# First MLP's output forms built from words held in SBUF, with own buffers for combining sums and an order planned with 315 GB/s of DMA

## The chip, the cores and the metric

The kernel runs on one core of a Trainium2 chip. Its metric is the device time of one execution in microseconds. The kernel before took 1105.91 us, the median of three runs (1105.8 to 1106.16).

## What is computed

Chunked attention (32 queries see 8 memory slots and a window of 56 keys and values) over 4 x 768 tokens and 8 heads is followed by two MLPs, 512 to 2048 to 512 wide, on all 3072 tokens. The inputs are float32; the kernel takes the weights of both MLPs as 64-bit words.

```python
for c in range(nc):
    scores = scale * np.matmul(q_c, k_full.transpose(0, 1, 3, 2))
    a = np.exp(scores - np.max(scores, axis=-1, keepdims=True))
    a = a / (np.sum(a, axis=-1, keepdims=True) + 1e-09)
    out[:, :, c_start:c_end] = np.matmul(a, v_full)
x = out.transpose(0, 2, 1, 3).reshape(B * S, H * D)
h = x @ w_in;  x = (h * (1.0 / (1.0 + np.exp(-h)))) @ w_out
h = x @ w2_in; r = np.maximum(h, 0.0); y = (r * r) @ w2_out
```

## The kernel before

**Numbers.** Every float32 operand of a matmul is kept as a high and a low part, and a product is three matmuls (low by high, high by low, high by high). A weight arrives as 64-bit words in a tile `wraw`; `words` makes a float32 tile `wu` of it with two passes on ScalarE (L621, L626, the second into a tile `wr`) and two on VectorE (L630, L636). `high` and `low` then split `wu` into the two parts.

**Stages.** The 3072 tokens are six blocks of 512. In the first two blocks the first MLP runs plainly (`mlp`: `hidden` L947 to L949, `back` L992 to L994); meanwhile its weights are converted (`convert`, block 0) and stay in SBUF: `w_in` in `i0` to `i15`, `w_out` as high and low parts in `o0` to `o9`, `u0` to `u2`. In the other four blocks (`first`, `front1`) the product with `w_out` is a block scheme with seven products for eight, per pair of 128-wide slices of the hidden layer: the sums of the left side are made per pair (`sums`, `split`), and the right side ("forms") is prepared once. The second MLP (`second`, `front`, `visit`) uses such a scheme for both of its products; its forms are prepared while the first MLP runs.

**The first MLP's output forms.** In `convert`, `keep_words` (L723) stores the `wu` tile of every `w_out` slice to the DRAM tensor `w1s` in two halves. In block 1, `convert_out(0, k)`, for each of the eight pairs k, loads the words of its two slices back into `wu` tiles (L759, four loads a pair), makes four differences (`diff`, L777), and stores the results to `w1s` (L824). `load_pair` (L1431) later loads a pair's six forms for each of the four blocks; the seventh form of all pairs is fetched by `hold_fourth` (L1403), split once into `o3` to `o6`, and the parts are stored to `w1h` (L1413), from where the last of the four blocks is served.

**The second MLP's weights.** Sixteen jobs, eight `stage_forms` and eight `convert_second` in turn, each load two `wraw` tiles, make words and differences, and store forms (`w2i` L891, `w2s` L811; seven stores of 256 KB in a `convert_second`). Which pair's step starts a job stands in `WORK0` for block 1 and in `WORK` for the blocks after it; in a block of `first` a job is due `LATER` = 20 us behind the step's time.

**Combining.** After a block of the seven-product scheme `combine` adds the products up from PSUM: a copy on ScalarE (L1484), then additions on VectorE (L1489), into four tiles of the pool `wr`, which `words`, the differences and the evictions of the first two blocks use too.

**What sets the order.** Nothing is issued when it is written: every step is a `Piece` with costs per engine, a due time, what it follows, the buffers it makes and uses, and `Graph.order` plans all of them with a list scheduler and emits them in the planned order, which fixes the order of every engine's queue. An engine runs its queue strictly in order, so an instruction that waits holds up all behind it. SyncE ("SP") issues all transfers. In the planner a transfer takes its bytes at `PIPE` MB/us on one pipe and lands `LANDING` us later; a step with two engines allowed goes to the cheaper one that is free.

```python
PIPE, LANDING, SPARE, DENSE, QUEUE = 0.34, 1.9, 3.0, 40.0, 1.5
...
pipe = max(pipe, p.end) + p.size / self.PIPE / 1e6
p.end = pipe + self.LANDING
```

Of the kernel before, what the change touches and what calls it, by code (L numbers as in the profile page):

```python
# [13 lines left out]
F32 = mybir.dt.float32  # L14
# [6 lines left out]
ALU = mybir.AluOpType  # L21
# [12 lines left out]
DM = H * D  # L34
DFF = 2048
P = 128
# [3 lines left out]
ON_PE = 2  # L40
AHEAD, SOON, SLOP = 15.0, 12.0, 2.0
FORMS1, FORMS2, LATER = (1, 2, 4, 5, 7), (0, 2, 4), 20
WORK0, WORK = (2, 4, 6), ((0, 1, 3, 4, 5), (2, 3, 4, 5), (2, 3, 4, 5))
UC = UG * GC // 2
QW, KW, VW = UC * CHUNK, UC * KC, UC * (D + 1)
UW = QW + KW + VW
# [10 lines left out]
HALF2 = T2 // 2  # L57
PAIRS = FT // 2
# [41 lines left out]
class Graph:  # L100
    HOP, DRAIN = 0.15, 0.2
    TABLE = 1.3
    PIPE, LANDING, SPARE, DENSE, QUEUE = 0.34, 1.9, 3.0, 40.0, 1.5

    def __init__(self):
        self.pieces, self.tags = [], {}
# [126 lines left out]
def chunk_attention_two_mlps(ctx, tc, units, weights, out):  # L233
# [17 lines left out]
        pool(tag)  # L251
    for tag, n in (
        ("rq", 1), ("rv", 2), ("pr", 1), ("pts", 1), ("xq", 3), ("x0", 1), ("x1", 1), ("g", 3), ("wraw", 2),
        ("wu", 4), ("wr", 4), ("nm", 3), ("sm", 4),
    ):
        pool(tag, n)
    for tag, n in (("acc", 4), ("ph", 2), ("sc", 2)):
# [2 lines left out]
    y1 = dram.tile([KT, P, NT], F32, name="y1")  # L260
    bounce = dram.tile([(NB - ON_PE) * HP * 2, P, GC, UG * CHUNK], F32, name="bounce")
    turns = iter(range((NB - ON_PE) * HP * 2))
    w1s = dram.tile([PAIRS, P, NF + 1, HALF2], F32, name="w1s")
    w1h = dram.tile([PAIRS, P, 2, HALF2], F32, name="w1h")
    w2i = dram.tile([PAIRS, P, NF, HALF2], F32, name="w2i")
    w2s = dram.tile([PAIRS, NF, P, 2, HALF2], F32, name="w2s")
# [1 line left out]
    def f(ap):  # L268
        return ap.bitcast(F32)

    def take(b, shape, dtype, name=None):
        b.tile = pools[b.tag].tile(shape, dtype, tag=b.tag, name=name or b.tag)
        return b.tile
# [379 lines left out]
    def convert(i, c):  # L653
# [64 lines left out]
        if c:  # L718
            w_kept[i] = []
            for half, part in enumerate(PLACES[i % 2]):  # L720
                def keep_words(e, half=half, part=part):
                    hs = slice(half * HALF2, (half + 1) * HALF2)
                    nc.sync.dma_start(out=w1s[i // 2, :, part], in_=wu.tile[:, hs])  # L723

                w_kept[i].append(G.add({"SP": 0.45}, due + 4, keep_words, [d], uses=[wu],
                                       size=P * HALF2 * 4))
# [17 lines left out]
    def convert_out(l, k, due):  # L744

        got, stored = {}, []
        for n in range(2):
            if l:
                wraw, at = load_words(k + n * PAIRS, 1, due)
                at.release = due - 25  # L750
                wu, at = words(1, k + n * PAIRS, 1, due, wraw, 0, at)
                got[n] = wu, [at]
            else:
                wu, i, at = G.buf("wu"), 2 * k + n, []
                for half, place in enumerate(PLACES[n]):
                    def load(e, wu=wu, half=half, place=place):
                        t = wu.tile if half else take(wu, [P, DM], F32)
                        hs = slice(half * HALF2, (half + 1) * HALF2)
                        nc.sync.dma_start(out=t[:, hs], in_=w1s[k, :, place])  # L759

                    at.append(G.add({"SP": 0.45}, due - 6, load, [*w_kept[i], *at[:half]],
                                    new=[wu] * (1 - half), uses=[wu] * half, size=P * HALF2 * 4))
                    at[-1].release = due - 12
                    stored.append(w_kept[i][half])
                got[n] = wu, at
        (ua, da), (ub, db) = got[0], got[1]
        z = [G.buf("wr"), G.buf("wr")]
# [4 lines left out]
        def diff(to, left, right, after, new):  # L772

            def emit(e):
                if new:
# [3 lines left out]
                )  # L779

            return G.add({"DVE": 0.42, "POOL": 0.75}, due + 1, emit, after, port=True,
                         new=[z[to[0]]] * new, uses=[ua, ub] + [z[to[0]]] * (not new))

        def b(src, half):
            return lambda: halves(src.tile)[:, half]
# [610 lines left out]
    def hold_fourth(due):  # L1396
        for k in range(0, PAIRS, 2):
# [14 lines left out]
            def store(e, k=k, w=w):  # L1412
# [3 lines left out]

            w_half[k] = [G.add({"SP": 0.45}, due + 40 + k, store, [d], uses=[w],
                                   size=4 * P * HALF2 * 4)]
            for i in range(2):
                held_fourth[k + i] = (w, i, d)  # L1420

# [52 lines left out]

    def combine(b, due):

        y = [G.buf("wr") for _ in range(4)]
        t1, u2, u3, y22 = y

        def done(n):  # L1480
# [288 lines left out]
```

## Time and profile before

| | us |
|---|---|
| median of 3 runs (1105.8 to 1106.16) | 1105.91 |
| the profiled execution's own time | 1104.76 |
| its span, first to last instruction | 1102.7 |
| TensorE (PE) busy | 1071.5 (97% of the span) |
| VectorE (DVE) busy | 823.5 (75%) |
| ScalarE (ACT) busy | 598.2 (54%) |
| GpSimd (POOL) busy | 230.6 (21%) |
| bytes moved, mean rate | 262.96 MB, 238 GB/s |

Busy time is the union of an engine's instructions. The matmuls are pipelined, so two neighbours overlap in the records: 12 matmuls of 512 columns take 2.8 us at the full clock (one starts 0.23 us after the other) and 5.1 us at half of it (0.43 us). The granted clock is shown as a share of 2.4 GHz; 0.50 is 1.2 GHz. The program's stages by time: start, to 34 us; blocks 0 and 1 of the first MLP, to about 231 us; its four other blocks, to about 607 us; the second MLP, to the end.

### The profile page before, as it was taken

Reading aid. Unit: us, or ns where it says so; the run is one execution under the profiler, and the core shown is the slowest. Engines: PE = TensorE matmul, PEld = TensorE weight load, DVE = VectorE, ACT = ScalarE, POOL = GpSimd, SP = SyncE. Lnnn points to the kernel's source line nnn. Section 1 sums busy time; section 2 is a strip of 40 time slices with the busy share of each in tenths; the row PEclk is TensorE's granted clock in tenths of the full one; section 3 lists DMA queues with packets and bytes.
Section 4 is the critical chain, followed back from the end, with each engine's and each line's share of the span. In section 5 each row is a group of like instructions: output and inputs, shape, how many; then the busy total and the mean of one; then the engine's idle time right before and its main releaser. Section 6 shows DMA issues by size and latency. Waiting matters only on the chain.

```text
span 1102.7 us, 25401 instructions
## 1 busy us (share of the span) xinstructions
PE 1071.5 (97%) x10060; PEld 980.5 (89%) x10060; DVE 823.5 (75%) x1621; ACT 598.2 (54%) x1102; POOL 230.6 (21%) x216
## 2 busy tenths in 40 slices
PE   6899999989998999999999999999999999999998
PEld 4677777768887888888889999999999999999998
DVE  4787755548789888887987887777777777777766
ACT  2788844437866758576676444334335335334333
POOL 0111102203334223411200321311221221211200
PEclk8799999998999999999999999999999999999999
DMA  7875898998888978866854585765765765766675
GB/s 270 298 258 193 259 290 287 312 311 273 284 279 276 311 250 272 276 223 213 271 201 157 196 262 172 244 211 165 262 202 183 242 210 180 226 208 215 203 222 173
DMA packets 145814, 262.96 MB, mean 238 GB/s; under 512 B 12704, under 2 KB 57888, under 8 KB 145696
## 3 DMA queue, kind: packets, MB, share of 16 engines
q1 hardware_dynamic: 145696, 261.34, 72.5%
q8 instruction: 79, 1.29, 0.5%
q14 instruction: 39, 0.32, 0.1%
HBM read 207.81 MB, written 53.48 MB: 237 GB/s over the span
## 4 chain that ended last, share of the span: by engine, by line
PE 79%; DMA 10%; DVE 5%; issue 2%; ACT 2%; SPq 1%; POOL 0%; ACTq 0%; DVEq 0%
PE out L1325 33%; PE pp L1145 21%; PE ph L947 6%; PE ph L948 6%; PE ph L949 6%; DMA turned<-bounce 2%; DMA w1s<-t 2%; DMA w<-w1s 2%; DMA raw<-units 2%; PE po L548 1%; PE acc L992 1%; PE acc L994 1%; PE acc L993 1%; PE sc L414 1%; DMA w2i<-wr 1%
## 5 line engine op out<-in xcount | busy, mean ns | idle before, releaser
L1145 PE MATMUL pp<-xs,forms 128*128 128x256 f32 x2016 | 274.2, 282 | 0.2 <-DVE kept L1171 0.2
L1325 PE MATMUL out<-w,g 128*128 128x256 f32 x2016 | 272.9, 283 | 1.3 <-DMA w<-w2s 0.6
L1325 PEld LDWEIGHTS out<-w,g 128*128 128x128 f32 x2016 | 255.7, 191 | 1.9 <-DVE y L1489 1.1
L1145 PEld LDWEIGHTS pp<-xs,forms 128*128 128x128 f32 x2016 | 253.8, 189 | 0.4 <-DVE kept L1171 0.4
L1203 ACT CAST g<-sums 128x512 fp32r<-128x512 f32 x240 | 148.2, 618 | 125.1 <-PE out L1325 109.1
L1207 DVE TENSOR_TENSOR g<-sums,g 128x512 fp32r<-128x512 f32 x202 | 156.0, 775 | 50.6 <-ACT g L1203 49.9
L1325 PE MATMUL out<-g,w 128*128 128x256 f32 x1344 | 175.3, 286 | 5.4 <-ACT y L1484 3.1
L1325 PEld LDWEIGHTS out<-g,w 128*128 128x128 f32 x1344 | 168.7, 191 | 10.9 <-ACT y L1484 3.5
L947 PE MATMUL ph<-x,i 128*128 128x512 f32 x384 | 155.6, 405 | 5.0 <-DVE pr L498 5.0
L1162 ACT ACTIVATE sums<-pp 128x256 f32<-128x256 f32 x192 | 73.7, 384 | 159.9 <-PE pp L1145 139.8
L948 PE MATMUL ph<-x,i 128*128 128x512 f32 x384 | 153.4, 399 | 0.0
L949 PE MATMUL ph<-x,i 128*128 128x512 f32 x384 | 153.2, 399 | 0.0
L1188 POOL TENSOR_TENSOR sums<-sums 128x256 f32<-128x256 f32 x55 | 46.6, 852 | 277.8 <-DVE sums L1188 236.5
L947 PEld LDWEIGHTS ph<-x,i 128*128 128x128 f32 x384 | 73.4, 191 | 22.1 <-issue 5.4
L1181 DVE SCALAR_TENSOR_TENSOR sums<-sums 128x256 f32<-128x256 f32 x144 | 67.2, 474 | 31.6 <-ACT sums L1162 29.6
L949 PEld LDWEIGHTS ph<-x,i 128*128 128x128 f32 x384 | 73.4, 191 | 17.6
L948 PEld LDWEIGHTS ph<-x,i 128*128 128x128 f32 x384 | 73.6, 192 | 15.5
L1207 POOL TENSOR_TENSOR g<-sums,g 128x512 fp32r<-128x512 f32 x38 | 49.9, 1315 | 170.8 <-ACT g L1203 163.5
L1188 DVE TENSOR_TENSOR sums<-sums 128x256 f32<-128x256 f32 x185 | 77.5, 437 | 7.2 <-ACT sums L1285 3.7
L1382 ACT CAST w<-w 128x512 fp32r<-128x512 f32 x100 | 60.6, 617 | 39.1 <-DMA w<-w1s 26.2
L1388 DVE TENSOR_TENSOR w<-w,w 128x512 fp32r<-128x512 f32 x76 | 58.5, 780 | 24.1 <-ACT w L1382 23.6
L630 DVE SCALAR_TENSOR_TENSOR wr<-wu,wr 128x512 int32<-128x512 int32 x64 | 46.2, 732 | 19.8 <-ACT wr L626 18.0
(109 smaller groups left out, 1312.6 us busy)
## 6 DMA issues: line engine op xcount, KB each, us to landing
w<-w2s SPq DMA_DIRECT2D x120, 512.0 KB, 4.0
w<-w1s SPq DMA_DIRECT2D x32, 768.0 KB, 5.4
w<-w2s SPq DMA_DIRECT2D x96, 256.0 KB, 3.1
wraw<-weights SPq DMA_DIRECT2D x44, 512.0 KB, 5.6
raw<-units SPq DMA_DIRECT2D x20, 768.0 KB, 6.3
w2s<-ws SPq DMA_DIRECT2D x56, 256.0 KB, 3.7
raw<-units SPq DMA_DIRECT2D x20, 520.0 KB, 5.9
bounce<-squares SPq DMA_DIRECT2D x32, 256.0 KB, 4.5
```

The costliest lines, as they stand in the source:

```text
L947: nc.tensor.matmul(o, w[:, 1, ws], x[:, 0, kt], start=(kt == 0), stop=False)
L948: nc.tensor.matmul(o, w[:, 0, ws], x[:, 1, kt], start=False, stop=False)
L949: nc.tensor.matmul(o, w[:, 0, ws], x[:, 0, kt], start=False, stop=(kt == KT - 1))
L1145: nc.tensor.matmul(o[:, at], w[:, a, ws], t[:, c, kt], start=first and kt == 0 and r == 0, stop=kt == 1 and r == 2, skip_group_check=True,)
L1162: nc.scalar.activation(t[:, to], q.bank[bank].tile[:, h], func)
L1181: nc.vector.scalar_tensor_tensor(t, t, 0.0, t, op0=ALU.max, op1=ALU.mult)
L1188: engine[e].tensor_tensor(q.t.tile[:, to], a[0].tile[:, a[1]], b[0].tile[:, b[1]], op=op)
L1203: nc.scalar.copy(take(g, [P, 2, 2, HALF2], F32R, "g2")[:, :, 0], read())
L1207: engine[e].tensor_tensor(t[:, :, 1], read(), f(t[:, :, 0]), op=ALU.subtract)
L1325: nc.tensor.matmul(out_, held[:, ms], moving, start=first and r == 0 and (m == 0 or alone is not None), stop=last and r == 2, skip_group_c ...
L1382: nc.scalar.copy(take(w, [P, m, 2, HALF2], F32R, "w2")[:, :, 0], raw.tile[:, at:at + m])
L1388: engine[e].tensor_tensor(t[:, :, 1], raw.tile[:, at:at + m], f(t[:, :, 0]), op=ALU.subtract)
```

## The change

`convert_out(0, k)` no longer loads the words: `whole` adds the high and low part of `w_out`, which are in SBUF, into a `wu` tile, one instruction per slice, on VectorE or GpSimd (16 in all). The half of a slice that only this load needed is no longer stored, and `w1s` is smaller by it. `combine` takes two of its four tiles from a new pool `y` with two buffers, and `wr` goes from four to three. The stores of `w1h` may be planned 250 us behind their due time at the earliest. `PIPE` and `LANDING` become 0.315 and 2.2. Each block has four jobs for the second MLP (block 1 had three, the block after it five). The fourth difference is also marked as a user of both of its inputs' tiles.

```diff
-WORK0, WORK = (2, 4, 6), ((0, 1, 3, 4, 5), (2, 3, 4, 5), (2, 3, 4, 5))
+WORK0, WORK = (1, 3, 5, 6), ((2, 3, 4, 5), (2, 3, 4, 5), (2, 3, 4, 5))
...
-    PIPE, LANDING, SPARE, DENSE, QUEUE = 0.34, 1.9, 3.0, 40.0, 1.5
+    PIPE, LANDING, SPARE, DENSE, QUEUE = 0.315, 2.2, 3.0, 40.0, 1.5
...
-        ("wu", 4), ("wr", 4), ("nm", 3), ("sm", 4),
+        ("wu", 4), ("wr", 3), ("y", 2), ("nm", 3), ("sm", 4),
...
-    w1s = dram.tile([PAIRS, P, NF + 1, HALF2], F32, name="w1s")
+    w1s = dram.tile([PAIRS, P, NF, HALF2], F32, name="w1s")
...
             for half, part in enumerate(PLACES[i % 2]):
+                if part == NF:
+                    continue
+
                 def keep_words(e, half=half, part=part):
...
-                wu, i, at = G.buf("wu"), 2 * k + n, []
-                for half, place in enumerate(PLACES[n]):
-                    def load(e, wu=wu, half=half, place=place):
-                        t = wu.tile if half else take(wu, [P, DM], F32)
-                        hs = slice(half * HALF2, (half + 1) * HALF2)
-                        nc.sync.dma_start(out=t[:, hs], in_=w1s[k, :, place])
-
-                    at.append(G.add({"SP": 0.45}, due - 6, load, [*w_kept[i], *at[:half]],
-                                    new=[wu] * (1 - half), uses=[wu] * half, size=P * HALF2 * 4))
-                    at[-1].release = due - 12
-                    stored.append(w_kept[i][half])
+                wu, i = G.buf("wu"), 2 * k + n
+
+                def whole(e, wu=wu, i=i):
+                    w = f(out_words(i))
+                    engine[e].tensor_tensor(
+                        take(wu, [P, DM], F32), w[:, 0], w[:, 1], op=ALU.add
+                    )
+
+                at = [G.add({"DVE": 0.70, "POOL": 1.30}, due - 1, whole, [w_done[i, 1]],
+                            new=[wu], uses=[w_out[i]], port=True)]
+                at[0].release = due - 12
+                stored += w_kept[i]
...
-                         new=[z[to[0]]] * new, uses=[ua, ub] + [z[to[0]]] * (not new))
+                         new=[z[to[0]]] * new, uses=[ua, ub] + (z if to == (1, 1) else [z[to[0]]] * (not new)))
...
+            w_half[k][0].release = due + 250
...
-        y = [G.buf("wr") for _ in range(4)]
+        y = [G.buf("y"), G.buf("y"), G.buf("wr"), G.buf("wr")]
```

Since the planner lays out everything anew, instructions move on every engine. Three places follow, where TensorE waits in the profile of before. Lines of the changed kernel are numbered 3 to 5 higher.

The first is VectorE about 20 us into the first block of the seven-product scheme. `nm` and `pr` are the maxima and the scores of an attention unit, which free the two PSUM banks `sc`; `wu` and `wr` belong to a conversion for the second MLP. Before:

```order
L630 SCALAR_TENSOR_TENSOR wr_3252<-wu_3215,wr_3252 128x512
L438 TENSOR_REDUCE nm_3268<-sc_3218 128x4
L636 SCALAR_TENSOR_TENSOR wu_3215<-wu_3215,wr_3252 128x512
L630 SCALAR_TENSOR_TENSOR wr_3263<-wu_3255,wr_3263 128x512
L498 TENSOR_TENSOR pr_3284<-sc_3218,nm_3268 128x4x64
L438 TENSOR_REDUCE nm_3268<-sc_3219 128x4
L498 TENSOR_TENSOR pr_3284<-sc_3219,nm_3268 128x4x64
L636 SCALAR_TENSOR_TENSOR wu_3255<-wu_3255,wr_3263 128x512
```

The same unit in the changed kernel:

```order
L1211 TENSOR_TENSOR g2_3210<-sums_3188,g2_3210 128x2x256
L438 TENSOR_REDUCE nm_3259<-sc_3213 128x4
L498 TENSOR_TENSOR pr_3267<-sc_3213,nm_3259 128x4x64
L438 TENSOR_REDUCE nm_3259<-sc_3214 128x4
L498 TENSOR_TENSOR pr_3267<-sc_3214,nm_3259 128x4x64
L1036 COPY y_3288<-acc_2149 128x512
L604 TENSOR_TENSOR x1_3269<-turned_3191,x1_3269 128x512
```

The conversion's four instructions no longer stand among those that free the banks; that conversion is now the fourth job of block 1, and stands earlier.

The second is ScalarE at the start of the next block, where `combine` copies the first product out of PSUM (L1484, then L1489). Before:

```order
L621 ACTIVATE wu_4608<-wraw_4471 128x512
L626 ACTIVATE wr_4624<-wraw_4471 128x512
L800 CAST ws_4629<-wu_4553 128x256
L1285 ACTIVATE sums_4631<-ph_4580 128x2x256
L505 ACT_TABLE_LOAD
L505 ACTIVATE pr_4567<-pr_4567 128x512
L800 CAST ws_4639<-wu_4608 128x2x256
L1484 COPY y_4643<-out_3358 128x512
```

Changed:

```order
L621 ACTIVATE wu_4467<-wraw_4388 128x512
L1207 CAST g2_4507<-kept_3200 128x2x256
L626 ACTIVATE wr_4511<-wraw_4388 128x512
L1489 COPY y_4526<-out_3346 128x512
L1386 CAST w2_4537<-w2_4443 128x2x256
L1207 CAST g2_4547<-kept_3200 128x2x256
L1386 CAST w2_4557<-w2_4443 128x2x256
```

The copy moved from behind the second `wraw` tile of a conversion, a table load and the exponential to a place ahead of them, two `hidden` products earlier on TensorE.

The third is GpSimd at the start of the block after that: `g2` are low parts of the left side, `w2` those of the forms. Before:

```order
L1207 TENSOR_TENSOR g2_6099<-sums_5833,g2_6099 128x2x256
L1388 TENSOR_TENSOR w2_6084<-w2_5870,w2_6084 128x2x256
L1388 TENSOR_TENSOR w2_6088<-w2_5870,w2_6088 128x2x256
L1207 TENSOR_TENSOR g2_6127<-sums_5833,g2_6127 128x2x256
L1207 TENSOR_TENSOR g2_6230<-sums_5994,g2_6230 128x2x256
```

Changed:

```order
L781 TENSOR_TENSOR t_6001<-wu_5951,t_6001 128x256
L781 TENSOR_TENSOR t_6095<-wu_5951,wu_5895 128x256
L1211 TENSOR_TENSOR g2_6066<-sums_5801,g2_6066 128x2x256
L1211 TENSOR_TENSOR g2_6111<-sums_5801,g2_6111 128x2x256
L1192 TENSOR_TENSOR sums_5973<-sums_5973 128x256
L808 TENSOR_TENSOR ws_6080<-wu_5951,ws_6080 128x2x256
```

The two subtractions for the forms (now `w2_5943`, `w2_5947`) have moved to VectorE, earlier in the program, and nothing stands between the two `g2` of the block's first pair.

## Rows read from the trace of the kernel before

**Rows 1.** The page's part 1: busy us, share of the span, instructions of each engine.

```profile
PE 1071.5 (97%) x10060; PEld 980.5 (89%) x10060; DVE 823.5 (75%) x1621; ACT 598.2 (54%) x1102; POOL 230.6 (21%) x216
```

**Rows 2.** Stretches of 50 us: busy us (instructions) by engine, PE clock, DMA share, GB/s.

```profile
200.00:250.00 50.00, 45.19 (x433) 35.62 (x432) 24.20 (x53) 21.68 (x37) 6.95 (x9) 0.98 0.97 310
300.00:350.00 50.00, 46.90 (x512) 41.11 (x511) 44.57 (x85) 35.84 (x63) 16.40 (x14) 0.97 0.82 276
450.00:500.00 50.00, 46.90 (x455) 41.52 (x454) 40.27 (x85) 31.43 (x57) 11.35 (x12) 0.97 0.68 233
700.00:750.00 50.00, 50.00 (x421) 50.00 (x421) 37.17 (x72) 17.98 (x37) 10.10 (x9) 1.00 0.65 202
```

**Rows 3.** Waits of PE: line, waited for: us in total, times, longest.

```profile
PE ph L947 <- DVE pr L498: 5.0, 2, 4.8
PE sc L414 <- DVE wr L630: 3.6, 1, 3.6
PE out L1325 <- ACT y L1484: 3.1, 1, 3.1
PE out L1325 <- POOL g L1207: 2.2, 1, 2.2
```

**Rows 4.** The three short stretches at half clock behind waits, columns as in rows 2.

```profile
248.50:255.20 6.70, 5.84 (x14) 4.63 (x15) 6.03 (x11) 6.30 (x12) 3.79 (x3) 0.50 0.32 123
347.50:350.80 3.30, 3.00 (x25) 2.78 (x33) 2.62 (x5) 2.22 (x5) 0.00 (x0) 0.50 0.71 207
453.30:456.60 3.30, 3.30 (x18) 3.30 (x17) 2.35 (x6) 1.04 (x2) 0.00 (x0) 0.50 1.08 341
```

**Rows 5.** Timeline of ACT and DVE, 243 to 249 us: start, us, instruction [idle before <-releaser].

```profile
243.99 0.66 ACT L621 ACTIVATE wu<-wraw 128x512 f32<-128x512 f32 x1 [5.33 <-DMA wraw<-weights]
...
245.23 0.69 DVE L630 SCALAR_TENSOR_TENSOR wr<-wu,wr 128x512 int32<-128x512 int32 x1 [5.41 <-ACT wr L626]
...
248.19 0.69 DVE L630 SCALAR_TENSOR_TENSOR wr<-wu,wr 128x512 int32<-128x512 int32 x1 [1.33 <-issue]
```

**Rows 6.** DMA issues, whole run: out<-in, times, size, median us to landing.

```profile
w1s<-wu SPq DMA_DIRECT2D x32, 128.0 KB, 4.1
wu<-w1s SPq DMA_DIRECT2D x32, 128.0 KB, 3.9
...
w2i<-wr SPq DMA_DIRECT2D x16, 256.0 KB, 4.5
...
w1h<-w SPq DMA_DIRECT2D x4, 512.0 KB, 5.4
```

**Rows 7.** Timeline of ACT, 342 to 348 us.

```profile
342.79 0.67 ACT L621 ACTIVATE wu<-wraw 128x512 f32<-128x512 f32 x1 [1.03 <-DMA wraw<-weights]
...
347.17 0.58 ACT L1484 COPY y<-out 128x512 f32<-128x512 f32 x1
```

**Rows 8.** Timeline of POOL, 447 to 453 us.

```profile
448.77 2.53 POOL L1388 TENSOR_TENSOR w<-w,w 128x512 fp32r<-128x512 f32 x2
451.26 1.46 POOL L1207 TENSOR_TENSOR g<-sums,g 128x512 fp32r<-128x512 f32 x1
```

**Rows 9.** The start, 28 to 35 us: SP, DVE, PE timelines, then landing times of L383's loads.

```profile
28.09 0.38 SPq L383 DMA_DIRECT2D raw<-units  x1
...
31.89 0.68 DVE L604 TENSOR_TENSOR x<-turned,x 128x512 fp32r<-128x512 f32 x1
...
33.09 0.69 DVE L712 TENSOR_TENSOR i<-wu,i 128x512 fp32r<-128x512 f32 x1
...
34.45 1.17 PE L414 MATMUL sc<-raw 64*32 64x64 f32 x64 [3.65 <-DVE wr L630]
...
DMA to landing us min/median/max: 6.2/7.1/8.0
```

**Rows 10.** Groups by line: shapes, count | busy us, mean ns | idle before.

```profile
L712 POOL TENSOR_TENSOR u<-wu,u 128x512 fp32r<-128x512 f32 x4 | 5.2, 1292 | 21.7 <-ACT u L708 21.7
...
L712 DVE TENSOR_TENSOR o<-wu,o 128x512 fp32r<-128x512 f32 x3 | 2.1, 690 | 1.9 <-ACT o L708 1.9
```

**Rows 11.** Waits of ACT's word instructions: us in total, times, longest.

```profile
ACT wr L626 <- DMA w1s<-t: 3.5, 3, 2.5
```

## The prediction

> **What bounds the kernel now.** I read the shares of the engines first, then the table by stages, then PE's own waits, and last the timelines around each wait. PE is busy for 97% of the span [rows 1], and from about 610 us to the end it is busy without a break: a stretch there shows 50.00 of 50 us at the full clock [rows 2]. Nothing that this change touches can shorten that part, since the matmuls stay the same. What can be won lies where PE is not at its peak: in the start, and in the first MLP, where a few stretches are short of 50 us and of the full clock [rows 2]. The list of PE's waits names four places [rows 3], and behind three of them the clock falls from 2.4 to 1.2 GHz after PE had idled, for the time that the stretches in [rows 4] show. So a wait costs its idle time and half of the busy time at half clock.
>
> The first is the wait of a `hidden` product at 244 us for the scores of an attention unit (4.8 us, [rows 3]). The reader should see in [rows 5] why DVE was late: it was idle for 5.41 us in front of an L630, which waited for ACT, which had waited 5.33 us for a `wraw` load. The reductions that free the bank stood behind that L630 in DVE's queue. A load was late because the 16 DMA engines were busy: 0.97 of the stretch, at 310 GB/s [rows 2]. The second, at 344 us, is `combine`'s copy, which began at 347.17 us, behind the words of a `wraw` tile for which ACT had waited until 342.79 us [rows 7]. The third, at 450 us, is a `g` that GpSimd could begin only at 451.26 us, after two L1388 of 2.53 us together [rows 8]. The fourth is the start: at 34.45 us a score for block 1 went ahead of the first `hidden` product [rows 9].
>
> **The change part by part.** *Start.* The wait at 34.45 us is put down to DVE's L630, but the score reads only a load; that load was issued at 28.09 us and took at least 6.2 us to land [rows 9], so it was the load that came last. In the changed order the score stands behind the first twelve matmuls of `hidden`, and the load is issued one place earlier. `hidden` then needs the last `x` part, which ended at 31.89 + 0.68 = 32.57 us, and the low part of `w_in`, which ended at 33.09 + 0.69 = 33.78 us [rows 9]; the changed order puts the latter ahead of the former. So PE starts between 32.6 and 33.8 us in place of 34.45: 0.7 to 1.9 us, and I take 1.7, since with that swap the last `x` ends the wait.
>
> *Words kept in SBUF.* 32 loads and 8 of 32 stores of 128 KB go [rows 6]: 4.2 + 1.0 MB, that is 13.5 and 3.4 us of the DMA engines at 310 GB/s [rows 2], and 40 issues of SP's queue. Added are 16 additions of 128x512; the order has 8 on GpSimd and 8 on DVE. The nearest rows are the subtractions of the same size: 1.29 us on GpSimd, 0.69 us on DVE [rows 10]. They lie between about 135 and 230 us, where DVE works half of the time (24.20 of 50 us, [rows 2]), and are hidden; without that cover they would cost at most 8 x 0.69 = 5.5 us on DVE.
>
> *Stores of `w1h` and jobs.* The four stores of 512 KB [rows 6] leave the stretch before 250 us, 2.1 MB or 6.8 us at 310 GB/s, and go to about 465 us, where the engines are busy 0.68 of the time [rows 2]. One conversion moves from the block after 230 us to the one before it: by its shapes two loads of 512 KB and seven stores of 256 KB, 2.9 MB. Block 1 thus loses 5.2 - 2.9 = 2.3 MB (the eight dropped stores lie just before it), and the stretch from 230 us loses 2.1 + 2.9 = 5.0 MB. Together with the changed order on DVE, where no instruction that hangs on a load stands between the score and its reductions, the wait at 244 us goes: 4.8 us, and of 5.84 us at half clock [rows 4] 2.9 us: 7.7 us. Its lower bound is nothing (DVE's queue has other conversions ahead, which now belong to block 1).
>
> *Combining.* The copy takes a tile of its own pool and stands ahead of the table load and of the second tile's words. 3.1 us go [rows 3], and half of 3.00 us [rows 4]: 4.6 us. Late next would be the sums that need `wr` tiles, of which there are three now; the order has them where they were. *GpSimd at 450 us.* The two L1388 are now on DVE and earlier: 2.2 us [rows 3] and half of 3.30 us [rows 4], 3.9 us. DVE has no great reserve there (40.27 of 50 us, [rows 2]), which is why I do not count on more.
>
> *Planner's numbers.* 0.315 in place of 0.34 lies near the 310 GB/s of the full stretch [rows 2]; the planner no longer sets work that hangs on loads where they cannot have landed. No time of its own.
>
> *What comes new.* All queues are laid out anew, and between 230 and 500 us DVE is still busy for 44.57 and 40.27 of 50 us [rows 2], with conversions in ACT's and DVE's queues ahead of work that PE needs. Bounds: none, or a wait like the largest, 7.7 us, and more than once. I take one of the smallest of the three, 3.9 us.
>
> **Sum**, against the profiled execution's own 1104.76 us: 1.7 + 7.7 + 4.6 + 3.9 = 17.9 us go, 3.9 us come: 1104.76 - 17.9 + 3.9 = 1090.8 us. The median of the runs is 1.15 us above that execution, so 1091.9 us.
>
> **A rule against it.** The stretch from 200 to 250 us shows 0.97 of the engines' time at 310 GB/s [rows 2]. The Trainium skill, "DMA: Bandwidth & Descriptors", section "Bandwidth", gives 425 GB/s for one core alone with large transfers and a ceiling of 435 by its ports; by it the engines would have about a quarter to spare at 310 (an estimate from that page). The row differs: busy to 0.97; whether the transfers' size explains it no run here shows. The rule is behind the third rival below.
>
> **Rivals.** *All clean*: no new wait; 1105.91 - 17.9 = 1088.0 us. For it: block 1 and the stretch from 230 us lose 2.3 and 5.0 MB. Against it: the small waits of before came from the same queues.
>
> *The block starts stay*: the waits at 344 and 450 us have the same kind of cause, a conversion's work in front of what frees a bank, and a new order may put another one there. Only the start and 244 us are won: 1105.91 - 1.7 - 7.7 = 1096.5 us. For it: DVE's 44.57 of 50 us; against it: the order at both places.
>
> *The loads are not late for want of DMA time*: they land as late as before, with fewer bytes in flight too, and the wait at 244 us turns up behind the conversion's new place; the others go: 1105.91 - 1.7 - 4.6 - 3.9 = 1095.7 us. Against it stands the 0.97. (By that page's rule it would be so.)
>
> *As many waits as before*: about 1105.5 us; the change would do what it says and the planner's new order give it back.
>
> *Slower: three `wr` tiles.* Each of the sixteen jobs writes four of them in turn, words and differences, so the second word of a job now waits for a store of the job's predecessor to land: 4.5 us in the median [rows 6]. ACT waited for such stores three times, 3.5 us, with four tiles already [rows 11]. What ACT then holds up is what frees PE's banks. Each time would cost about 3.9 us as at 450 us; beyond 17.9 + 2.2 us it is slower, so from the sixth of sixteen jobs on: 1088.0 + 6 x 3.9 = 1111.4 us. For it: DVE and ACT have little reserve from 230 us on; against it: the planner knows the three tiles and counts landing later than before.
>
> **How the numbers follow.** Chances: forecast 0.43, all clean 0.22, block starts stay 0.12, loads late anyway 0.08, as many waits 0.06, slower 0.09. A measurement of this kernel tells about 0.2% (2.2 us) from no change. Faster: 0.43 + 0.22 + 0.12 + 0.08 = 0.85; same 0.06; slower 0.09. The range goes from all clean with the start at its best and some of the smaller waits gone, 1085, to the block starts staying with one new wait, 1096.5 + 3.9 = 1100; left out are the last two cases, 0.15.
>
> **What would show it.** In the changed kernel's profile: the first `hidden` product before 33.8 us; the stretch from 200 to 250 us with fewer bytes and 50 us of PE; no wait of PE for L498, for `combine`'s copy or for a `g` of GpSimd, and the half clock only in the start and at one further place. Wrong: a wait of several us for ACT or DVE behind an L626 or L630 that waits for a store from `wr`; the DMA share still at 0.97 from 200 to 250 us; DVE at 48 of 50 us and PE waiting for it.

## The result and the profile after

The changed kernel took 1092.94 us, the median of four runs (1091.94 to 1097.13); the kernel before, beside it, 1105.86 us (four runs, 1103.66 to 1106.16). The ratio is 0.9895 (95% interval 0.9866 to 0.9924): faster by 1.05%. The forecast was 1091.9 us, in a range from 1085 to 1100. The profiled execution took 1092.37 us, 12.4 us less than the profiled execution before; its span is 1090.6 us.

Part 1 of its page answers to [rows 1]; its stretches answer to [rows 2] and [rows 4], with the same columns. The stretch from 438.7 us is the only one at half clock between the start and the last matmul:

```profile
PE 1067.3 (98%) x10060; PEld 977.0 (90%) x10060; DVE 820.9 (75%) x1626; ACT 598.9 (55%) x1102; POOL 244.5 (22%) x227
```

```profile
150.00:200.00 50.00, 50.00 (x516) 39.53 (x515) 35.40 (x76) 25.62 (x37) 15.38 (x14) 1.00 0.84 278
200.00:250.00 50.00, 50.00 (x527) 40.13 (x526) 33.10 (x70) 28.62 (x48) 15.62 (x16) 1.00 0.84 281
300.00:350.00 50.00, 48.74 (x542) 43.41 (x541) 42.78 (x83) 35.99 (x62) 15.42 (x16) 1.00 0.87 294
438.70:445.50 6.80, 5.97 (x28) 5.97 (x29) 3.96 (x7) 2.28 (x4) 1.31 (x1) 0.50 0.61 224
450.00:500.00 50.00, 50.00 (x484) 44.35 (x483) 40.14 (x80) 32.44 (x60) 12.24 (x10) 1.00 0.79 269
```

From 200 to 250 us PE now has no gap, at the full clock, and the DMA share is 0.84 in place of 0.97. The waits of PE answer to [rows 3]. Three of the four that stood there are gone, and of the fourth, for a `g` of GpSimd, 0.4 us of 2.2 are left. The longest behind the start is new, for an addition of `combine` (L1494):

```profile
PE out L1329 <- DVE y L1494: 4.1, 2, 2.9
PE ph L951 <- DVE i L712: 1.7, 1, 1.7
PE po L548 <- ACT sums L1289: 0.9, 2, 0.6
PE out L1329 <- POOL g L1211: 0.4, 1, 0.4
```

At the start (timelines of PE and DVE, [rows 9]) the first hidden product stands at 30.31 us in place of 35.55 us, and the score for block 1 runs behind its first twelve matmuls:

```profile
30.31 0.80 PE L951 MATMUL ph<-x,i 128*128 128x512 f32 x1 [1.68 <-DVE i L712]
...
35.73 0.93 PE L414 MATMUL sc<-raw 64*32 64x64 f32 x64
```

**The ledger of the two profiled executions.** Gone: at the start 35.55 - 30.31 = 5.24 us, less the 1.17 us of the score that only moved, 4.1 us; at 244 us 4.8 us and half of 5.84 us, 7.7 us; at 344 us 3.1 us and half of 3.00 us, 4.6 us; at 450 us 2.2 us and half of 3.30 us, 3.9 us [rows 3, 4, 9]. Sum: 20.3 us. Come: L1494 4.1 us, `g` on GpSimd 0.4 us and half of 5.97 us at half clock, 3.0 us: 7.5 us. The smaller waits behind the start sum to 2.6 us, before to 2.3 us (ScalarE's sums, L1289, are no newcomer: 0.9 us, before 0.8 us); with these 0.3 us it is 7.8 us. That leaves 12.5 us, against the 12.4 us measured.

The new waits are `combine`'s. Timelines of PE, DVE and GpSimd at 436 us:

```profile
439.53 2.71 PE L1329 MATMUL out<-g,w 128*128 128x256 f32 x11 [2.87 <-DVE y L1494]
...
435.05 0.69 DVE L1494 TENSOR_TENSOR y<-out,y 128x512 f32<-128x512 f32 x1
435.66 0.68 DVE L808 TENSOR_TENSOR ws<-t,ws 128x512 fp32r<-128x512 f32 x1
436.26 1.49 DVE L781 TENSOR_TENSOR t<-wu,t 128x256 f32<-128x256 f32 x1
437.67 1.21 DVE L1211 TENSOR_TENSOR g<-sums,g 128x512 fp32r<-128x512 f32 x1
438.80 1.28 DVE L1494 TENSOR_TENSOR y<-out,y 128x512 f32<-128x512 f32 x2
...
436.04 1.43 POOL L1211 TENSOR_TENSOR g<-sums,g 128x512 fp32r<-128x512 f32 x1 [0.28 <-ACT g L1207]
437.43 0.90 POOL L1192 TENSOR_TENSOR sums<-sums 128x256 f32<-128x256 f32 x1
```

The bank that PE needs is freed by the two L1494 that begin at 438.80 us, behind two instructions of a conversion (L808, L781) and a `g`. The last two of these three took nearly twice their time and more: at the like place in the block before, the same L781 took 0.42 us and the same L1211 0.68 us, and PE waited there for 1.25 us.

### The profile page after: what moved, and what is told of

It is laid out like the page before. It is cut to its first block, busy times and chain, and to the rows that moved or that the text cites. A ratio compares the mean times of both kernels' runs of the same rounds, so it can differ in the third digit from the quotient of the medians.

```text
span 1090.6 us, 25390 instructions
## 1 busy us (share of the span) xinstructions
PE 1067.3 (98%) x10060; PEld 977.0 (90%) x10060; DVE 820.9 (75%) x1626; ACT 598.9 (55%) x1102; POOL 244.5 (22%) x227
## 4 chain that ended last, share of the span: by engine, by line
PE 90%; DMA 4%; DVE 3%; issue 1%; ACT 1%; SPq 0%; DVEq 0%; ACTq 0%
PE out L1329 34%; PE pp L1149 21%; PE ph L951 8%; PE ph L953 8%; PE ph L952 8%; PE acc L996 3%; PE acc L998 3%; PE acc L997 3%; PE po L548 2%; PE sc L414 1%; DMA w<-w2s 1%; DMA w<-w1s 1%; DMA wraw<-weights 1%; DMA raw<-units 1%; DMA w2s<-ws 1%
## 5 line engine op out<-in xcount | busy, mean ns | idle before, releaser
L1211 DVE TENSOR_TENSOR g<-sums,g 128x512 fp32r<-128x512 f32 x203 | 160.8, 794 | 61.8 <-ACT g L1207 60.8
L1192 POOL TENSOR_TENSOR sums<-sums 128x256 f32<-128x256 f32 x58 | 45.9, 797 | 275.8 <-DVE sums L1192 221.7
L1192 DVE TENSOR_TENSOR sums<-sums 128x256 f32<-128x256 f32 x182 | 75.1, 431 | 9.8 <-ACT sums L1289 8.0
L1392 DVE TENSOR_TENSOR w<-w,w 128x512 fp32r<-128x512 f32 x78 | 55.9, 737 | 13.4 <-ACT w L1386 13.1
L1211 POOL TENSOR_TENSOR g<-sums,g 128x512 fp32r<-128x512 f32 x37 | 48.5, 1312 | 74.5 <-ACT g L1207 74.5
```

Of the source, the lines that this page charges most:

```text
L1192: engine[e].tensor_tensor(q.t.tile[:, to], a[0].tile[:, a[1]], b[0].tile[:, b[1]], op=op)
L1211: engine[e].tensor_tensor(t[:, :, 1], read(), f(t[:, :, 0]), op=ALU.subtract)
L1392: engine[e].tensor_tensor(t[:, :, 1], raw.tile[:, at:at + m], f(t[:, :, 0]), op=ALU.subtract)
```

## The experiments

The changed kernel has five separable parts: the words kept in SBUF, the planner's two numbers, the pool `y`, the later release of the `w1h` stores, the split of the jobs. A label with u_ is the changed kernel with one part undone, one with o_ the kernel before with one part alone; all these are planned anew. `o_plan`, `o_words` and `two` also carry the change's mark that makes the fourth difference a user of both tiles, which can move instructions too and was not tried alone. A label with h_ holds a kernel's planned order on every engine and moves or adds only what is named. My theory at the outset was that of the prediction: at 244 us a conversion in front of the reductions in VectorE's queue, with its loads late for want of DMA time.

### The parts undone one by one

**u_plan.** The planner's numbers back.

```diff
-    PIPE, LANDING, SPARE, DENSE, QUEUE = 0.315, 2.2, 3.0, 40.0, 1.5
+    PIPE, LANDING, SPARE, DENSE, QUEUE = 0.34, 1.9, 3.0, 40.0, 1.5
```

> The changed kernel with the planner's old numbers (0.34 and 1.9); all else as changed. Theory: the numbers by themselves set the order of the start, where the score stands ahead of the first hidden product again, and little else: the first hidden product about 35.5 us in place of 30.3 us, 1.2 us of which the score's matmuls only change places, so 1092.9 + 4 = about 1097 us, and no wait of several us near 244 us. Rival: the numbers are what keeps work that hangs on loads out of VectorE's queue where it can't have landed; then a wait like the 4.8 us at 244 us comes back too, 1097 + 7.7 = about 1104.7 us.

Measured: 1101.85 us beside 1106.69 us, ratio 0.9965 (0.9946 to 0.9985). About a third of the gain is left. The profiled execution took 1106.86 us, 5.0 us more than the median, so its waits add up to more than the median shows. In it the first hidden product came at 37.73 us. Some of PE's waits:

```profile
PE po L548 <- ACT sums L1289: 5.9, 9, 1.5
PE sc L414 <- DMA raw<-units: 4.4, 1, 4.4
PE out L1329 <- POOL g L1211: 2.6, 2, 2.0
PE ph L951 <- DVE pr L498: 1.5, 2, 1.3
```

The start and the wait for GpSimd's `g` are back, ScalarE's sums are late nine times (5.9 us, in the changed kernel 0.9), and the wait of a hidden product for L498 is back with 1.5 us, not with 4.8. It lies between theory and rival: more than the start, but not the large wait.

**u_words.** The words loaded back from DRAM.

```diff
-                at = [G.add({"DVE": 0.70, "POOL": 1.30}, due - 1, whole, [w_done[i, 1]],
...
+                    at.append(G.add({"SP": 0.45}, due - 6, load, [*w_kept[i], *at[:half]],
```

> The changed kernel with the words loaded back from DRAM as before (32 loads and 8 stores of 128 KB more, 5.2 MB, 16 additions less); all else as changed. In its order no instruction of a conversion that waits for a load stands between the scores and their reductions on VectorE near 244 us. Theory (VectorE's queue behind a late load made that wait): the DMA share from 150 to 250 us is back near 0.95, but TensorE does not wait there: 1093 to 1096 us. Rival (want of DMA time made it, whatever the order): loads land late and a wait of 4 us or more comes back between 200 and 260 us, 1092.9 + 7.7 = about 1100.6 us.

Measured: 1099.74 us, ratio 0.9940 (0.9915 to 0.9964): nearly half of the gain is lost, and the theory's 1093 to 1096 us was wrong. Its stretch from 200 to 250 us, and some of PE's waits:

```profile
200.00:250.00 50.00, 48.36 (x448) 38.22 (x448) 30.40 (x63) 25.54 (x42) 12.79 (x13) 1.00 0.94 307
```

```profile
PE out L1325 <- DVE y L1490: 6.4, 2, 3.5
PE po L548 <- ACT sums L1285: 2.9, 2, 1.9
PE sc L414 <- DVE xq L559: 1.1, 1, 1.1
```

By time it is the rival's 1100.6 us, but not by the rival's wait of 4 us and more: no hidden product waited for L498, the longest wait between 200 and 260 us was 1.9 us (L1285), and the waits for the sums of `combine` rose from 4.1 to 6.4 us.

**u_y.** Four `wr` tiles and no pool `y`.

```diff
-        y = [G.buf("y"), G.buf("y"), G.buf("wr"), G.buf("wr")]
+        y = [G.buf("wr") for _ in range(4)]
```

> The changed kernel with combine's four tiles from wr again, four of them, and no pool y; all else as changed. Theory: the copy that starts the sums stands behind the words again and TensorE waits for it once or twice: 3.1 us and half of 3.0 us each, 1097.5 to 1102 us. Rival: the waits at 340 and 436 us of the changed kernel come from the two tiles that are still taken from wr, and the copy is no later than they; then the own pool is worth nothing or less: 1090 to 1094 us.

Measured: 1089.96 us, ratio 0.9860 (0.9828 to 0.9892). The rival holds: the own pool is worth nothing that shows; the interval overlaps with the changed kernel's.

**u_rel.** The `w1h` stores early again.

```diff
-            w_half[k][0].release = due + 250
```

> The changed kernel without the later release of the w1h stores: 2.1 MB of stores go out before 250 us again; all else as changed. Theory (with the words kept in SBUF the DMA engines have room there, 0.84 of their time): within 2 us of the changed kernel, 1091 to 1095 us. Rival (the stretch is bound by DMA time): a wait of 3 us or more comes back between 200 and 260 us, 1097 us and more.

Measured: 1095.55 us beside 1105.78 us, ratio 0.9914 (0.9888 to 0.9940), not told apart from the changed kernel. It does not try the rival, though: in its trace the four stores were issued from 255.93 to 287.89 us, behind the stretch from 200 to 250 us (50.00 us of PE, DMA share 0.80). That there is room for them with the words in SBUF is shown by `two` below. The split of the jobs was not tried by itself.

### Order or bytes

**h_queue.** Kernel before, order held; four instructions go ahead on VectorE.

```diff
-L630, L438, L636, L630, L498, L438, L498, L636
+L438, L498, L438, L498, L630, L636, L630, L636
```

> The kernel before with its planned order held, except that on VectorE the four reductions and scores of the unit near 244 us (two L438, two L498) go ahead of the two L630 and the L636 that stood between them. Not a byte and no other instruction moves. Theory (VectorE's queue made the wait): the 4.8 us and half of the 5.84 us at half clock go, 1105.9 - 7.7 = 1098.2 us, and the DMA share of 200 to 250 us stays at 0.95 or more. Rival (loads are late for want of DMA time, and what hangs on them is late in any order): TensorE waits a few us further on for sums, words or a pair's forms, 1103 to 1106 us.

Measured: 1105.71 us beside 1105.78 us, ratio 1.0014 (0.9992 to 1.0036); the profiled execution took 1109.54 us, 3.8 us more than the median. No gain: the theory falls. The wait of this kernel's PE, then ACT's timeline:

```profile
PE out L1325 <- ACT y L1030: 3.9, 1, 3.9
```

```profile
247.65 0.66 ACT L621 ACTIVATE wu<-wraw 128x512 f32<-128x512 f32 x1 [5.07 <-DMA wraw<-weights]
...
257.26 0.57 ACT L1030 COPY y<-acc 128x512 f32<-128x512 f32 x1
```

The reductions were no longer late, and PE did not wait for them. But ScalarE waited 5.07 us for the same load, and the copy that empties a bank of block 1's results stood 9.6 us behind that in its queue. The wait turned up at 254 us with 3.9 us, and the half clock with it. A late load held up ScalarE's queue too, where no order of VectorE helps.

**h_bytes.** Kernel before, order held; the four stores of `w1h` go to the place on SP planned for 465 us (in the traces from 229, 230, 237 and 242 us to 479 to 484 us).

```diff
-w1h<-w (four times, between the transfers of 214 to 231 us of the plan)
+w1h<-w x4 (ahead of the first transfer behind 465 us of the plan)
```

> The kernel before with its planned order held, except that the four stores of w1h (512 KB each) go from 214 to 231 us to about 465 us on SP. Theory (the loads at 237 us are late for want of DMA time): the three stores issued ahead of them carried 1.6 MB, 5.1 us at 310 GB/s, so both loads land 3 to 5 us earlier and the wait at 244 us shrinks to under 1.5 us: 1105.9 minus 5 to 7 = 1099 to 1101 us. Rival (landing does not hang on these bytes): the wait at 244 us stays between 3.5 and 5 us, 1104 to 1107 us.

Measured: 1105.73 us beside 1105.76 us, ratio 1.000 (0.998 to 1.002); the profiled execution took 1109.03 us, 3.3 us more than the median. Neither theory nor rival. The wait at 244 us is gone: the stretch from 200 to 250 us has 50.00 us of PE and a DMA share of 0.87, and the loads took 5.4 and 6.4 us to land (before 6.8 and 9.2). That is not the bytes' work alone: PE also came there about 2.6 us later than before, behind a wait of 1.9 us at 188 us with its half clock (ScalarE's copy `kept`, just ahead of the two `wraw` tiles, began at 240.62 in place of 238.00 us). And behind the four stores in a row at 479 us ScalarE waited 6.25 us for a load of `w`, and PE 2.9 us for ScalarE's sums at 496 us, with half clock after it; the copy of `combine` was late by 3.4 us (before 3.1). With fewer bytes in this place the loads landed sooner; with the same bytes elsewhere the kernel took as long as before.

**o_words.** Kernel before with the words kept in SBUF alone.

```diff
+                if part == NF:
+                    continue
...
+                at = [G.add({"DVE": 0.70, "POOL": 1.30}, due - 1, whole, [w_done[i, 1]],
```

> The kernel before with the words kept in SBUF alone (32 loads, 8 stores less; 16 additions more); numbers, jobs, stores of w1h and tiles as before. Theory (bytes and numbers are both needed): the DMA share of 150 to 250 us falls under 0.9 and the wait at 244 us is at most 2 us, but the start is as before and several waits of about 1 us for ScalarE's sums stay: 1099 to 1103 us, neither as fast as the changed kernel nor as slow as before. Rival 1 (the bytes do it all): 1093 to 1096 us with the start's 3 us still to win. Rival 2 (bytes alone do nothing, as the numbers alone did nothing): 1104 us and more.

Measured: 1098.15 us beside 1105.76 us, ratio 0.9942 (0.9919 to 0.9964): 7.6 us, the sum of all that moved (PE's waits for ScalarE's sums, for one, rose from 0.8 to 3.2 us). This run is the clearest, since its order still has the two words among the scores and the reductions. Stretch, ACT and DVE:

```profile
200.00:250.00 50.00, 49.97 (x455) 39.58 (x454) 26.15 (x55) 25.25 (x43) 10.79 (x10) 1.00 0.88 284
```

```profile
240.53 0.70 ACT L621 ACTIVATE wu<-wraw 128x512 f32<-128x512 f32 x1 [0.51 <-DMA wraw<-weights]
...
241.81 0.69 DVE L630 SCALAR_TENSOR_TENSOR wr<-wu,wr 128x512 int32<-128x512 int32 x1 [0.62 <-ACT wr L626]
242.42 0.42 DVE L438 TENSOR_REDUCE nm<-sc 128x4 f32<-128x256 f32 x1
242.76 0.68 DVE L636 SCALAR_TENSOR_TENSOR wu<-wu,wr 128x512 int32<-128x512 int32 x1
244.50 0.69 DVE L630 SCALAR_TENSOR_TENSOR wr<-wu,wr 128x512 int32<-128x512 int32 x1 [1.06 <-ACT wr L626]
245.10 0.42 DVE L498 TENSOR_TENSOR pr<-sc,nm 128x256 f32<-128x256 f32 x1
```

The same sequence as in [rows 5], with ScalarE's wait 0.51 us in place of 5.33. The loads took as long to land as before (7.6 and 9.0 us). They were in time because SP issued them 4.2 us earlier (232.84 in place of 237.07 us), while PE came there 1.4 us later (that `kept` copy at 239.37 us). PE waited for none of it.

**o_plan.** Kernel before with the planner's new numbers alone.

```diff
-    PIPE, LANDING, SPARE, DENSE, QUEUE = 0.34, 1.9, 3.0, 40.0, 1.5
+    PIPE, LANDING, SPARE, DENSE, QUEUE = 0.315, 2.2, 3.0, 40.0, 1.5
```

> The kernel before with the planner's new numbers alone (0.315 and 2.2). Its order has the first hidden product ahead of the score at the start, and no words of a conversion between the scores and their reductions on VectorE near 244 us. Theory (the two numbers carry most of the change, by the order that they set): the start is some 3 to 4 us earlier and the wait at 244 us is gone though the DMA share there stays over 0.9: 1105.9 - 3.5 - 7.7 = 1094.7 us. Rival (the numbers help only where bytes have gone too): waits of 2 us and more for conversions' loads turn up elsewhere between 200 and 460 us, 1100 us and more.

Measured: 1108.33 us beside 1105.78 us, ratio 1.0028 (1.0006 to 1.0049): no gain, rather a loss. The start was won (first hidden product at 32.07 us), but not the stretch:

```profile
200.00:250.00 50.00, 48.40 (x446) 37.97 (x444) 28.59 (x61) 25.57 (x43) 6.49 (x7) 1.00 0.96 315
```

```profile
PE out L1325 <- ACT y L1030: 4.9, 1, 4.9
PE out L1325 <- DVE y L1032: 3.1, 1, 3.1
```

Again evictions of block 1 were late, as in h_queue, but not behind a late load: from 225 to 265 us no instruction of ScalarE waited for a transfer. The copy on ScalarE (L1030, 253.29 us) stood behind a conversion's split that had waited 1.85 us for VectorE's L636, and the one on VectorE (L1032, 262.94 us) behind a split (L804) that had waited 1.08 us for ScalarE's part of it.

**h_load.** Changed kernel, order held; 40 transfers of 128 KB go between SP's own.

```diff
+                    nc.sync.dma_start(out=more[n], in_=weights[1, n % FT, :, :DM // 4])
```

> The changed kernel with its planned order held on every engine, and 40 transfers of 128 KB from DRAM to DRAM, whose result nothing uses, put between SP's transfers from about 140 to 226 us: the 5.2 MB and 40 issues that the change took away, without their place in the order. Theory (the missing bytes are what lets loads land in time): the DMA share from 150 to 250 us goes from 0.84 to 0.93 or more, and waits of 2 to 5 us for conversions' loads or what stands behind them come back between 200 and 260 us: 1097 to 1101 us. Rival (the new numbers' order is enough by itself): no wait of more than 1 us there, 1092 to 1094 us.

Measured: 1112.92 us, ratio 1.0066 (1.0042 to 1.0089): 20 us more than the changed kernel and slower than the one before, beyond the theory's 1097 to 1101 us. But the DMA share, which the theory had at 0.93 or more, was 0.86 from 150 to 200 us and 0.80 from 200 to 250 us. So this run does not show a want of DMA time; the 40 issues also took SP's queue, 0.50 us each. The extra 5.2 MB are 17 us at 310 GB/s, and they are read and written in DRAM. PE waited 6.4 us at 230 us for a `g` on VectorE, which stood behind an `x` that waited for `turned`; the load of `turned` was issued only when its `bounce` store had landed, 6.2 us after its issue. Its PE waits (lines one higher):

```profile
PE ph L952 <- DVE g L978: 9.3, 3, 6.4
PE out L1330 <- DVE y L1495: 5.8, 2, 2.9
PE sc L415 <- ACT sums L1290: 2.2, 2, 2.0
```

**two.** Kernel before with two parts: words kept in SBUF and the new numbers.

```diff
+    PIPE, LANDING, SPARE, DENSE, QUEUE = 0.315, 2.2, 3.0, 40.0, 1.5
...
+                at = [G.add({"DVE": 0.70, "POOL": 1.30}, due - 1, whole, [w_done[i, 1]],
```

> The kernel before with two parts of the change, the words kept in SBUF and the planner's new numbers; jobs, stores of w1h and combine's tiles as before. Theory (these two carry the change: the bytes let loads land in time, worth 7.6 us alone, and the numbers are worth the start's 3 to 4 us and waits of about 1 us for ScalarE's sums once the bytes are gone): 1091 to 1095 us, no wait over 1.5 us between 200 and 260 us, the first hidden product by 33 us. Rival (the jobs and the later stores are needed too, since four of the words of a conversion stand between the scores and their reductions again in this order): a wait of 2 us and more near 244 us and 1096 to 1099 us.

Measured: 1096.11 us beside 1105.26 us, ratio 0.9908 (0.9880 to 0.9935), the interval overlaps with that of the whole change. By time it lies at the rival's edge, by the profile it is the theory: the first hidden product came at 30.63 us, and PE had 50.00 us from 200 to 250 us, with no wait for L498 there, though the four stores of `w1h` were issued from 211.53 to 234 us (DMA share 0.86). What it lacks most is the copy of `combine`, at 334 us:

```profile
PE out L1329 <- ACT y L1488: 3.6, 2, 3.3
```

### The new wait

**ring4.** The tiles of `wr` are handed out in the order in which the code asks for them, so a sum of `combine` may not take its tile before the differences of a job that was written down earlier have theirs. Here `combine`'s two are asked for ahead of the fourth step's job.

```diff
+            if q.k == 4 and q.b < len(WORK):
+                ringed[q.b] = [G.buf("wr"), G.buf("wr")]
             if q.b < len(WORK) and q.k in WORK[q.b]:
...
-        y = [G.buf("y"), G.buf("y"), G.buf("wr"), G.buf("wr")]
+        y = [G.buf("y"), G.buf("y"), *(ringed.pop(b, None) or [G.buf("wr"), G.buf("wr")])]
```

> The changed kernel with the two wr tiles of combine taken in the ring ahead of the fourth and later steps' jobs of the block, not behind them; all else as changed. Theory: the waits of the changed kernel at 340 us (1.25 us) and at 436 us (0.44 and 2.87 us, and 3.4 us of half clock's loss) come from sums that may not take a wr tile before the last job's differences have theirs; with that order of the ring TensorE waits for no sum there: 1092.9 - 1.3 - 3.3 - 3.4 = about 1085 us. Rival: VectorE has no room there whatever the ring's order, and the job that now goes behind the sums makes a wait of the same size for its own bank: 1091 to 1095 us.

Measured: 1092.11 us, ratio 0.9874 (0.9839 to 0.9908). PE no longer waits for any L1494, which agrees with the theory; but u_y, with the ring's old order and four `wr` tiles, waits only 0.4 us for it too, so the cause is not shown by this run alone. The time is that of the changed kernel within the interval. Where it went:

```profile
PE pp L1149 <- DVE kept L1175: 2.6, 1, 2.6
PE po L548 <- ACT sums L1289: 1.4, 2, 0.8
PE out L1329 <- DVE g L1211: 1.3, 2, 1.1
PE out L1329 <- POOL g L1211: 0.7, 1, 0.7
```

The wait for L1175 lies at 598 us, where the second MLP begins, with half clock for 3.4 us behind it; and this execution's start was 2.4 us later (32.74 us). The rival's end, by another mechanism: the wait moved.

**uy_ringall4.** As u_y, with all four tiles asked for ahead of the fourth step's job.

```diff
+            if q.k == 4 and q.b < len(WORK):
+                ringed[q.b] = [G.buf("wr") for _ in range(4)]
```

> The changed kernel with four wr tiles and no pool y, and combine's four tiles taken in the ring ahead of the jobs from the fourth step on. Theory: the kernel without the pool y (1090.0 us) had waits of 1.2, 1.3, 0.5 and 1.6 us at 341, 344, 438 and 440 us behind sums that came late; with the tiles taken early they go and nothing takes their place: 1090.0 - 4.6 = about 1085.4 us. Rival (as with the first ring order, what is won at the sums is given back at a later wait): 1089 to 1092 us.

Measured: 1091.58 us beside 1105.78 us, ratio 0.9880 (0.9854 to 0.9906). The half clock is gone from everything but the start and the last 0.7 us, and behind the start waits of 0.2 to 1.4 us are left (DVE's L1211 3.2 us in four). The rival holds. No version is shown to beat the changed kernel; u_y has the lowest median.

## Why the prediction was right, and which of its steps were not

The time was right to 1.0 us, and part of that is luck, since two errors cancelled: by the ledger 2.4 us more went than forecast (20.3 in place of 17.9), nearly all of it at the start, and 3.9 us more came (7.8 in place of 3.9). Step by step:

*The wait at 244 us*, 7.7 us: it went, with its half clock, as forecast [rows 3, 4]; that o_words alone gained 7.6 us is near, but a net of other waits. Half of its reason failed. I had put it on the bytes "together with the changed order on DVE"; h_queue shows the order on VectorE alone to be worth nothing, and o_words shows the wait gone in the old order. The cause is the landing of the loads, measured against the moment at which PE needs what stands behind them; a late load held ScalarE's and VectorE's queues, and whatever bank was freed behind them was late. The third rival, that loads land late whatever the bytes and the wait turns up elsewhere, falls: no such wait is left in the changed kernel or in o_words. But half of it held in o_words, where each load took as long to land as before and was only issued sooner; only h_bytes shows shorter landings with fewer bytes, and h_load, at a DMA share of 0.80, decides nothing here.

The Trainium skill, "DMA: Bandwidth & Descriptors", section "Bandwidth", gives besides the 425 GB/s a limit of about 358 GB/s of HBM for each core, which binds between HBM and SBUF. The trace does not settle on that one either. Three stretches of the changed kernel in which the DMA engines were busy throughout, by 10 us (last columns: DMA share, GB/s):

```profile
10.00:20.00 10.00, 5.30 (x237) 4.07 (x238) 4.95 (x17) 1.78 (x3) 0.18 (x1) 0.94 1.04 399
160.00:170.00 10.00, 10.00 (x105) 7.92 (x104) 8.91 (x23) 5.19 (x8) 3.66 (x4) 1.00 1.04 357
230.00:240.00 10.00, 10.00 (x105) 7.85 (x104) 4.97 (x11) 5.72 (x11) 3.65 (x3) 1.00 1.03 366
```

The last two lie within about 2% of the lower limit, the first 11% above it. What speaks against a quarter to spare is therefore the share, 0.97, and not the 310 GB/s; whether another mix of transfers would have moved more at that share no run here shows.

*Planner's numbers*, "No time of its own": wrong. In the whole change, undoing them costs 0.9965 against 0.9895, about 0.7% or 8 us; added to the words alone they gained less, 0.3% (`two` 0.9908, o_words 0.9942, the intervals overlap); without the words' part they cost 0.3% (o_plan). They set the order of the start too, which I had priced separately.

*Start*, 1.7 us: right that the score gives way, the size too small, and the last `x` did not end the wait. Five executions with the score first (the one before and four others) began it at 34.45 to 36.63 us, 35.3 in the mean (in the four others the profile puts the wait there down to the load, as I had read it); nine with the new order had the first hidden product at 30.31 to 33.11 us, 32.1 in the mean. The gain is 3.3 us in the mean and 4.1 us in this pair. In all nine the first product waited for the low part of `w_in` (L712; in the changed kernel 29.57 + 0.69 = 30.26 us), and the last `x` ended behind it (30.17 + 0.68 = 30.85 us). I had taken the DVE rows of one execution as fixed. They lie behind matmuls at half clock, and how long that lasts differs: of the nine, the two with 3.4 us of it ahead of 29 us began at 30.31 and 30.63 us, the others, with 8.6 us and more, at 31.79 to 33.11 us. So a part of this pair's 4.1 us is the luck of one execution.

*Stores of `w1h`*, counted as 6.8 us of DMA time: they left the stretch, but `two` has them in it and no wait. The stores, the jobs and the pool together are worth something while the words are still loaded (u_words 0.9940, o_plan 1.0028, which differ by these three); which of them no run isolates, and with the words kept `two` is not told apart from the whole change. *Combining*, 4.6 us, and *GpSimd at 450 us*, 3.9 us: both waits went (of the second 0.4 us are left), and most of their time came back in the same blocks. The tiles of its own were not what brought the copy forward: u_y has none and no wait for the copy, and `two`, which waits 3.3 us for it, differs from u_y only in the split of the jobs and the release of the stores. *What comes new*, 3.9 us: 7.8 us. I had named it ("Late next would be the sums that need `wr` tiles") and then not priced it: 4.1 us of L1494 and 3.0 us of half clock. The fifth rival, stores that hold the three `wr` tiles, did not come: no wait of ScalarE's L626 for a store leads to one of PE's new waits. The additions were about as priced: 0.68 to 0.69 us for seven of the eight on VectorE and 1.23 us for the other, 1.39 us in the mean on GpSimd.

Still open: whether the words' part works by its bytes or by its 40 issues on SP. h_bytes moved four issues and 2.1 MB, and the loads landed sooner, which speaks for bytes; in o_words they were only issued sooner, which speaks for SP's queue; h_load added both.

## What to carry to other kernels

Where several in-order queues hang on one late load, moving the instruction that waits may only move the wait to the next bank that is freed behind it, as here from 244 to 254 us; look first for transfers that can go, the cheapest being those whose data are still in SBUF in another form. Try a planner's numbers again when the load on the resource that they describe has changed: here the same two numbers lost 0.3% with the words still loaded, and gained 0.3% (`two`) to 0.7% (u_plan) with the words kept. When a sum of gains counts waits that share one scarce buffer ring, price the next user of that ring as well.

## What the runs showed of the hardware

VectorE and GpSimd held each other up. In the rows at 436 us above, L781 of VectorE began 0.22 us after GpSimd's L1211 and ended at 437.75 us, 0.28 us after that (437.47): 1.49 in place of 0.42 us; the L1211 behind it took 1.21 in place of 0.68 us beside GpSimd's L1192. Together 1.6 us, over half of PE's 2.87 us. In the block before it was GpSimd that lost: its L1211, begun 0.03 us after VectorE's L1211 at 340.60 us, took 1.79 us, the one before it 1.30 us. The Trainium skill, "SBUF — State Buffer", section "Terms", says that the two share a pair of ports which one holds for a whole instruction while the other blocks; these rows agree.

By the profile SP, too, waited for landings that its next transfer does not read. From 100 to 250 us of the kernel before (waits of SP: line, waited for; us, times, longest), among others:

```profile
SPq L473 <- DMA raw<-units: 2.7, 3, 1.6
SPq L811 <- DMA wraw<-weights: 2.4, 1, 2.4
SPq L473 <- DMA wraw<-weights: 2.2, 3, 0.9
SPq L465 <- DMA wraw<-weights: 2.0, 1, 2.0
```

L465 stores `squares` and has no need of `wraw`. Waits put down to a landing other than that of `bounce`, which L473 reads, sum to 20.2 us there and to 5.4 us in the changed kernel; a few of them are for a buffer that the landing frees. The profile infers these causes from semaphore events, so that a transfer in flight holds up unrelated issues is not shown, and what would limit their number no run here isolates.
